# Contracting every matmul of an attention-and-expert kernel over 64 partitions, in two row tiles at once

## The chip, the cores and the metric

The kernel runs on one core of a Trainium2 chip. The metric is the device time of one execution in microseconds (us). Every time given for a kernel is the median of all its executions, slow ones included. A run called "fast" here is one within 1.5% of the fastest of the same kernel; ratios use fast runs alone.

The engines are named as the profile names them: PE is TensorE's matmuls, PEld its weight loads, ACT is ScalarE, DVE is VectorE, POOL is GpSimd, SP is the engine that issues DMA transfers. A matmul multiplies a stationary operand (loaded by a weight-load instruction; the page of the kernel after counts 9098 of each) with a moving one. Both lie across the partitions that it contracts over, 128 or 64 in these kernels, called rows below. A "64-row" matmul uses one half of them, and two of them in opposite halves run at once in these traces (they start 3 to 4 nanoseconds apart, and a pair of 512 columns takes 216, as long as one 128-row matmul): those halves are the two row tiles of the title.

## The reference

```python
# q, k, v: (batch 8, heads 8, sequence 1152, head 64), float32
q_pool = q.reshape(B, H, S // 2, 2, D).mean(axis=3)            # 576 queries per head
scores = (q_pool @ k.transpose(0, 1, 3, 2)) / np.sqrt(D)
attn   = softmax(scores)
x      = (attn @ v).transpose(0, 2, 1, 3).reshape(4608, 512)
out    = np.maximum(x @ w1, x @ w2) @ w_out                    # 512 -> 1024 -> 512
```

The kernels use max(a, b) = relu(a - b) + b: with wd = w1 - w2 and w21 = w2 @ w_out, computed once, the second part is relu(x @ wd) @ w_out + x @ w21. It is called the expert part below.

## The kernel before

The kernel records all its operations in one list, in an order chosen by a small planner at build time, and then emits each engine's share. An operation waits on semaphores for what it depends on. Two heads (a "head pair") are handled together, 32 pairs in all.

Three kinds of TensorE work matter here. The scores contract over the head's 64 elements, so they always used 64 rows: head 0 of the pair in the upper half, head 1 in the lower, side by side.

```python
sps = [psum([P, 2, 512], f"sps{g}") for g in range(3)]     # three score buffers
fb  = [psum([P, 512], f"fb{g}") for g in range(2)]         # two "lanes" for all other work

def one(e, half, t, lo, n, col):                           # scores
    h = half * 64
    return e.matmul(sps[r][:, half, col:col + n],
                    kT[ks][h:h + 64, t, :], qpT[qs][h:h + 64, lo:lo + n], start=True, stop=True)
...
# ScalarE: one exponential of 128 x 1024 per key tile (nine of them, and two rest groups)
return e.activation(eta[es][:, :, g, :], sps[r][:, :, :], EXP, scale=scale)
```

The value matmuls (attention times v, with a column of ones for the row sums, 65 columns) and the two expert layers (mostly 512 columns) contract over all 128 partitions:

```python
def chunk(half, sb):                                       # values: 9 matmuls of 65 columns
    def go(e, m):
        for t in range(NT):
            last = e.matmul(fb[m][:, sb * 66:sb * 66 + 65],
                            eta[es][:, half, t, sb * P:(sb + 1) * P], vE[vs][:, t, half, 0:65],
                            start=(t == 0), stop=(t == NT - 1))
        return last
...
last = e.matmul(fb[m][:, 0:size], wd[:, ct, ft * P:(ft + 1) * P], xT[:, ct, n0:n1],
                start=(ct == 0), stop=(ct == NC_ - 1))     # expert layer 1; layer 2 is alike
```

While attention runs, the planner puts scores first, in bursts of two or three groups, and fills the gaps with value and expert units. What of the expert part is left when the scores are done is the "tail".

The softmax here doesn't subtract the row's maximum and nothing guards it: scores larger than these inputs give would overflow.

Of the kernel before, what the change touches and what calls it, by code (L numbers as in the profile page):

```python
# [9 lines left out]
EXP = mybir.ActivationFunctionType.Exp  # L10
ALU = mybir.AluOpType


class Plan:

# [28 lines left out]
    def when(self, eng, r=(), w=(), after=()):  # L44

        t = self.free.get(eng, 0.0)
        for d in self.deps(r, w, after)[0]:
            p = self.ops[d]
            if p["eng"] != eng or p["dma"] is not None:
                t = max(t, p["seen"] + 0.05)  # L50
        return t

    def op(self, eng, fn, r=(), w=(), dma=None, cost=0.1, mode="f", after=(), solo=False):
# [7 lines left out]
        t = self.when(eng, r, w, after)  # L61
# [4 lines left out]
        else:  # L66
            if eng == "PE" and mode != self.mode:
# [5 lines left out]
                             seen=seen, end=self.free[eng], solo=solo))  # L73
# [7 lines left out]
    def solve(self):  # L81
# [3 lines left out]
        for n, o in enumerate(ops):  # L85
# [3 lines left out]
            for d in sorted(o["deps"], reverse=True):  # L89
                p = ops[d]  # L90
                if p["dma"] is None:
                    if p["eng"] == eng and (eng == "PE" or d not in o["raw"]):
                        continue
                    key = p["eng"]
                else:
                    key = ("dma", p["dma"])
                if kn.get(key, -1) >= d:
                    continue
                o["waits"].append(d)
                for k, v in p["know"].items():  # L100
                    if kn.get(k, -1) < v:
                        kn[k] = v
                kn[key] = max(kn.get(key, -1), d)
# [39 lines left out]
class Job:  # L143


    def __init__(self, kind, units, evac, done=None, nb=None):
        self.kind, self.units, self.evac, self.done = kind, units, evac, done
        self.nb = nb


def bass_funnel_attn__then__act_maxout2_kernel(
# [14 lines left out]
    QP = 64  # L166
    QU = SQ // QP
    NA = 512
    NB = SQ - NA
    NCH = NA // P  # L170
# [5 lines left out]
    NBLK = NTOK // 512  # L176
    assert D == 64 and S == NT * P and SQ == QP * QU and QU == NT and C == H * D and E == 512
    assert NB == 64 and NTOK % 512 == 0 and NT == 9
    scale = 0.5 / float(D) ** 0.5

    ctx = ExitStack()
    with ctx:
# [10 lines left out]
        qp = [sbuf([QP, QU, 2, D], BF16, f"qp{s}") for s in range(2)]  # L193
# [4 lines left out]
        eta = [sbuf([P, 2, NT, NA], BF16, f"eta{s}") for s in range(2)]  # L198
        etb = [sbuf([P, NT, 2, NB], BF16, f"etb{s}") for s in range(2)]
        rc = [sbuf([P, 6], FP32, f"rc{s}") for s in range(2)]  # L200
# [13 lines left out]
        osb = [stage[:, NC_ * F + s * E:NC_ * F + (s + 1) * E] for s in range(3)]  # L214

        sps = [psum([P, 2, 512], f"sps{g}") for g in range(3)]
        fb = [psum([P, 512], f"fb{g}") for g in range(2)]

        plan = Plan()
        op = plan.op  # L220

# [19 lines left out]
        def load_q(i):  # L241
# [3 lines left out]
                q[b, h0:h0 + 2, :, :].rearrange("h (p r) d -> (h p) (r d)", p=QP)),  # L245
# [22 lines left out]
        def cast_q(i):  # L268
            s, r = i % 2, i % 3
            for half in range(2):  # L270
                a = qraw[r][half * QP:half * QP + QP, :, :, :]
                op("POOL", lambda g, half=half, a=a: g.tensor_tensor(  # L272
                    qp[s][:, :, half, :], a[:, :, 0, :], a[:, :, 1, :], ALU.add),
                    r=[f"qraw{r}"], w=[f"qp{s}.{half}"], cost=1.4,
                    solo=half == 1)
# [7 lines left out]
        def unit(r, cost, go, mode="f"):  # L283

            def plan_it(m):
                op("PE", lambda e: go(e, m), r=r, w=[f"f{m}"], cost=cost, mode=mode)
            return r, plan_it, cost
# [4 lines left out]
        def qtrans(i):  # L292
            s = i % 2

            def go(e, m):
                mb = fb[m][:, :].bitcast(BF16)
                for u in range(QU):
                    last = e.transpose(  # L298
                        mb[:, u * QP:(u + 1) * QP],
                        qp[s][:, u, :, :].rearrange("p h d -> p (h d)"), ident[0:QP, 0:QP])  # L300
                return last

            def evac(m):
                mb = fb[m][:, :].bitcast(BF16)
                dve(lambda e: e.tensor_copy(qpT[s][:, :], mb[:, 0:SQ]),
                    [f"f{m}"], [f"qpT{s}", f"f{m}"], 0.4)
            return Job("q", [unit([f"qp{s}.0", f"qp{s}.1", "ident"], 0.3, go, "s")], evac, ("q", i))

        def ktrans_pe(i):
            s = i % 2  # L310
            v3 = i % 3
            jobs = []
            for lo, hi in ((0, 5), (5, NT)):
                def go(e, m, lo=lo, hi=hi):
                    mb = fb[m][:, :].bitcast(BF16)
                    for t in range(lo, hi):
                        last = e.transpose(
                            mb[:, (t - lo) * P:(t - lo + 1) * P],
                            kbf[s][:, t, :, :].rearrange("p h d -> p (h d)"), ident[:, :])
                    return last  # L320

                def evac(m, lo=lo, hi=hi):
                    mb = fb[m][:, :].bitcast(BF16)
                    dve(lambda e: e.tensor_copy(
                        kT[v3][:, lo:hi, :].rearrange("p t x -> p (t x)"),
                        mb[:, 0:(hi - lo) * P]),
                        [f"f{m}"], [f"kT{v3}", f"f{m}"], 0.7)
                jobs.append(Job("q", [unit([f"kbf{s}", "ident"], 0.055 * (hi - lo), go)], evac,
                                ("k", i) if lo else None))
            return jobs  # L330

        def av_jobs(i):
# [6 lines left out]
            def chunk(half, sb):  # L339
                def go(e, m):  # L340
                    for t in range(NT):
                        last = e.matmul(  # L342
                            fb[m][:, sb * 66:sb * 66 + 65],
                            eta[es][:, half, t, sb * P:(sb + 1) * P],
                            vE[vs][:, t, half, 0:65],
                            start=(t == 0), stop=(t == NT - 1))
                    return last
                return unit([f"eta{es}.{t}" for t in range(NT)] + [f"vE{vs}"], 0.275, go)

            def rest():  # L350
                def go(e, m):
                    for t in range(NT):
                        last = e.matmul(  # L353
                            fb[m][:, 4 * 66:4 * 66 + 131],
                            etb[es][:, t, :, :].rearrange("p h c -> p (h c)"),
                            vE[vs][:, t, :, :].rearrange("p h c -> p (h c)")[:, 0:131],
                            start=(t == 0), stop=(t == NT - 1))
                    return last
                return unit([f"etb{es}.{NT}", f"etb{es}.{NT + 1}", f"vE{vs}"], 0.53, go)

            def norm(half):
                def evac(m):
                    n = 6 if half == 0 else 4
                    c = c0 + half * D
                    a = fb[m]
                    dve(lambda e: e.reciprocal(  # L366
                        rc[half][:, 0:n],
                        a[:, 0:n * 66].rearrange("p (j c) -> p j c", c=66)[:, :, 64:65]),
                        [f"f{m}"], [f"rc{half}"], 0.13)
                    dve(lambda e: e.tensor_tensor(  # L370
                        xnat[xs][:, 0:NCH, c:c + D],
                        a[:, 0:NCH * 66].rearrange("p (j c) -> p j c", c=66)[:, :, 0:D],
                        rc[half][:, 0:NCH].unsqueeze(2).to_broadcast([P, NCH, D]),
                        ALU.mult),
                        [f"f{m}", f"rc{half}"],
                        [f"xn{xs}.{j}.{h0 + half}" for j in range(NCH)]
                        + ([f"f{m}"] if half else []), 0.38)
                    if half == 0:
                        dve(lambda e: e.tensor_scalar_mul(
                            xnat[xs][0:64, NCH, c:c + D], a[0:64, 264:264 + D],  # L380
                            rc[0][0:64, 4:5]), [f"f{m}", "rc0"], [f"xn{xs}.{NCH}.{h0}"], 0.2)
                        dve(lambda e: e.tensor_scalar_mul(  # L382
                            xnat[xs][0:64, NCH, c + D:c + 2 * D], a[64:P, 330:330 + D],
                            rc[0][64:P, 5:6]), [f"f{m}", "rc0"],
                            [f"xn{xs}.{NCH}.{h0 + 1}", f"f{m}"], 0.2)
                return evac

            last = ("x", b) if i % NHP == NHP - 1 else None
            return [
                Job("a", [chunk(0, sb) for sb in range(NCH)] + [rest()], norm(0)),  # L390
                Job("a", [chunk(1, sb) for sb in range(NCH)], norm(1), last)]
        gcount = [0]

        def scores(i, g):
# [3 lines left out]
            r = gcount[0] % 3  # L398
            gcount[0] += 1

            def one(e, half, t, lo, n, col):
                h = half * 64
                return e.matmul(  # L403
                    sps[r][:, half, col:col + n],
                    kT[ks][h:h + 64, t, :],
                    qpT[qs][h:h + 64, lo:lo + n],
                    start=True, stop=True)

            if g < NT:
                def pe(e):  # L410
                    one(e, 0, g, 0, NA, 0)
                    return one(e, 1, g, 0, NA, 0)

                def act(e):
# [494 lines left out]
```

## Time and profile before

The median was 418.46 us in the runs before the change (414.5 to 418.68).

| reading | value |
|---|---|
| span of the profiled execution | 415.9 us |
| PE busy | 379.6 us (91%) |
| ACT busy | 314.4 us (76%) |
| first exponential starts, last ends | 13.1 us, 341.7 us |
| tail after the last exponential | 74 us |
| steps between 64-row and 128-row matmuls, in the built order | 321 |

Three parts of the page of the kernel before: busy time of each engine with its instructions; two DMA queues (packets, MB, share of 16 engines' time); the chain of work that ended last.

```profile
PE 379.6 (91%) x4846; PEld 203.6 (49%) x4905; DVE 156.3 (38%) x355; ACT 314.4 (76%) x370; POOL 164.9 (40%) x136
...
q1 hardware_dynamic: 81552, 85.05, 74.0%
q8 instruction: 38, 0.62, 0.6%
...
PE 80%; DVE 8%; ACT 6%; issue 2%; DMA 1%; POOL 1%; another core or an unknown queue 0%
```

TensorE is the limit: it is busy 91% of the time and holds 80% of the chain. q8 is the queue whose packets the profile calls "instruction", 38 in the whole run.

The stretches view of the kernel before: window, its length, busy us (and instructions) of PE, PEld, DVE, ACT, POOL, then the granted TensorE clock, the DMA share and GB/s.

```profile
100.00:200.00 100.00, 96.86 (x1333) 50.97 (x1349) 36.51 (x90) 91.58 (x106) 48.63 (x38) 1.00 0.79 209
200.00:300.00 100.00, 96.69 (x1416) 53.18 (x1435) 38.45 (x96) 93.55 (x110) 50.66 (x40) 1.00 0.96 255
...
342.00:416.00 74.00, 67.64 (x393) 31.66 (x399) 20.46 (x36) 8.60 (x17) 0.00 (x0) 1.00 0.32 67
```

During attention both TensorE (97%) and ScalarE (92 to 94%) are near full; then TensorE works alone for 74 us.

The timeline of PE, 201 to 204 us: start, length, line and operation, number of matmuls. (L342 values, L403 scores, L581 expert layer 2.)

```profile
201.26 1.26 PE L342 MATMUL fb<-vE,eta 128*128 128x65 bf16 x36
202.46 0.82 PE L403 MATMUL sps<-qpT,kT 64*128 64x512 bf16 x6
203.44 0.38 PE L581 MATMUL fb<-w,xT 128*128 128x512 bf16 x1 [0.16 <-issue]
203.65 1.13 PE L342 MATMUL fb<-vE,eta 128*128 128x65 bf16 x32
```

This is the pattern that the change attacks: TensorE goes from 128 rows (L342) to 64 rows (L403) and back. In the records of this trace each such step costs about 94 nanoseconds (ns) more than a step without it (a value matmul is followed by a score matmul after 125 ns instead of 30). What TensorE does in these 94 ns, the trace doesn't show.

Two lines of the waits view of the kernel before: who waited for what, total us, times, longest.

```profile
ACT eta L415 <- PE sps L403: 34.3, 31, 11.1
...
PEld fb L342 <- issue: 14.4, 34, 0.8
```

ScalarE is starved for 34 us in all, 11.1 of them at the start. Idle time put down to "issue" (nothing that the profile shows was being waited for) never lasts over 0.8 us on TensorE.

### The profile page before, as it was taken

The page shows a single profiled execution, that of the slowest core. Times are in us where ns is not written, and L with a number is a line of the kernel's source. Part 1 is how long each engine was busy: PE and PEld are TensorE (multiplying, and loading weights), DVE is VectorE, ACT ScalarE, POOL GpSimd, SP SyncE. Part 2 cuts the span into 40 slices and gives each one's busy share as a digit, 9 for nine tenths or more (in the row PEclk, how much of TensorE's full clock was granted, in tenths as well). Part 3 has the DMA queues.
Part 4 walks back from the last instruction along what each step waited for, and adds up shares of the span by engine and source line. Part 5 has one row for each costly group of instructions (what it writes and reads, how often), then busy time and mean ns, then how long its engine had stood idle before and what let it go on. Part 6 is the DMA issues. An engine that isn't in the chain of part 4 may idle for free.

```text
span 415.9 us, 11123 instructions
## 1 busy us (share of the span) xinstructions
PE 379.6 (91%) x4846; PEld 203.6 (49%) x4905; DVE 156.3 (38%) x355; ACT 314.4 (76%) x370; POOL 164.9 (40%) x136
## 2 busy tenths in 40 slices
PE   0787897899999999999999999999999999999996
PEld 0355544545365536545555545555555554344442
DVE  1224738344233533244334433344333444432210
ACT  1788997899989997999799999999999980011121
POOL 5982643654346534644165536452751000000000
PEclk9988998999999999999999999999999999999999
DMA  8999997796499949974999899849964203423223
GB/s 297 403 401 391 401 283 182 155 333 159 78 344 249 277 91 315 328 225 59 303 283 240 131 307 305 267 64 325 296 138 93 46 2 65 96 50 76 64 61 66
DMA packets 81600, 85.76 MB, mean 206 GB/s; under 512 B 54416, under 2 KB 54416, under 8 KB 81552
## 3 DMA queue, kind: packets, MB, share of 16 engines
q1 hardware_dynamic: 81552, 85.05, 74.0%
q8 instruction: 38, 0.62, 0.6%
q14 instruction: 10, 0.08, 0.1%
HBM read 62.91 MB, written 9.44 MB: 174 GB/s over the span
## 4 chain that ended last, share of the span: by engine, by line
PE 80%; DVE 8%; ACT 6%; issue 2%; DMA 1%; POOL 1%; another core or an unknown queue 0%
PE fb L581 23%; PE fb L342 17%; PE sps L403 17%; PE fb L549 15%; ACT eta L415 5%; PE fb L353 4%; PE fb L298 2%; DVE wd L488 2%; PE fb L516 1%; DVE stage L598 1%; DMA qraw<-in_q_dram 1%; DVE xnat L370 1%; DVE xnat L382 1%; DVE wo L483 1%; POOL qp L272 1%
## 5 line engine op out<-in xcount | busy, mean ns | idle before, releaser
L415 ACT ACTIVATE eta<-sps 128x1024 bf16<-128x1024 f32 x288 | 269.6, 1047 | 35.0 <-PE sps L403 34.3
L272 POOL TENSOR_TENSOR qp<-qraw 64x576 bf16<-64x576 f32 x64 | 90.8, 1419 | 60.9 <-PE fb L298 54.2
L403 PE MATMUL sps<-qpT,kT 64*128 64x64 bf16 (+1 forms) x1152 | 104.6, 290 | 7.3 <-ACT eta L415 5.5
L342 PEld LDWEIGHTS fb<-vE,eta 128*128 128x128 bf16 x2304 | 79.4, 98 | 37.3 <-issue 14.4
L342 PE MATMUL fb<-vE,eta 128*128 128x65 bf16 x2304 | 88.7, 194 | 6.1 <-DVE xnat L382 3.1
L549 PE MATMUL fb<-xT,wd 128*128 128x512 bf16 (+2 forms) x304 | 76.3, 358 | 3.1 <-issue 1.3
L581 PE MATMUL fb<-wo,stage 128*128 128x512 bf16 (+1 forms) x275 | 76.5, 380 | 1.7 <-issue 1.0
L564 DVE TENSOR_SCALAR stage<-fb 128x512 bf16<-128x512 f32 (+2 forms) x68 | 44.4, 656 | 69.4 <-PE fb L549 69.0
L403 PEld LDWEIGHTS sps<-qpT,kT 64*128 64x128 bf16 x1152 | 31.2, 94 | 54.2 <-ACT eta L415 27.6
L279 POOL TENSOR_SCALAR vE<-vraw 128x1152 bf16<-128x1152 f32 x32 | 37.3, 1165 | 47.7 <-issue 35.0
L257 POOL TENSOR_SCALAR kbf<-kraw 128x1152 bf16<-128x1152 f32 x31 | 36.7, 1184 | 48.0 <-DMA kT<-kbf 47.3
L366 DVE RECIPROCAL rc<-fb 128x6 f32<-128x6 f32 x64 | 12.1, 189 | 114.0 <-PE fb L353 71.7
L549 PEld LDWEIGHTS fb<-xT,wd 128*128 128x128 bf16 x320 | 25.3, 97 | 37.2 <-DVE stage L564 6.0
L558 ACT ACTIVATE stage<-fb 128x288 bf16<-128x288 f32 (+1 forms) x12 | 5.7, 473 | 50.0 <-PE fb L549 50.0
L581 PEld LDWEIGHTS fb<-wo,stage 128*128 128x128 bf16 (+1 forms) x296 | 26.0, 98 | 30.3 <-issue 7.4
L581 PE MATMUL fb<-w,xT 128*128 128x512 bf16 (+1 forms) x130 | 37.3, 381 | 3.3 <-DVE stage L598 1.4
L427 ACT ACTIVATE etb<-sps 128x1024 bf16<-128x1024 f32 x64 | 38.8, 673 | 0.2
L598 DVE COPY stage<-fb 128x512 f32<-128x512 f32 (+1 forms) x32 | 22.1, 690 | 31.4 <-PE fb L581 31.1
L370 DVE TENSOR_TENSOR xnat<-fb,rc 128x256 bf16<-128x256 f32 x64 | 27.2, 424 | 2.2
L353 PE MATMUL fb<-vE,etb 128*128 128x131 bf16 x288 | 23.1, 226 | 0.0
L298 PE MATMUL fb<-ident,qp 64*128 64x64 bf16 x288 | 14.0, 192 | 9.8 <-POOL qp L272 8.8
L298 PEld LDWEIGHTS fb<-ident,qp 64*128 64x128 bf16 x288 | 10.7, 96 | 19.6 <-POOL qp L272 8.8
(27 smaller groups left out, 113.7 us busy)
## 6 DMA issues: line engine op xcount, KB each, us to landing
qraw<-in_q_dram SPq DMA_DIRECT2D x32, 576.0 KB, 7.0
kraw<-in_k_dram SPq DMA_DIRECT2D x32, 576.0 KB, 5.9
vraw<-in_v_dram SPq DMA_DIRECT2D x32, 576.0 KB, 8.1
out_dram<-stage SPq DMA_DIRECT2D x72, 128.0 KB, 2.5
xT<-in_moe_w_dram SPq DMA_DIRECT2D x1, 2048.0 KB, 15.6
stage<-in_moe_w_out_dram SPq DMA_DIRECT2D x1, 2048.0 KB, 19.3
stage<-in_moe_w_dram SPq DMA_DIRECT2D x1, 2048.0 KB, 17.4
xT<-xnat SPq DMA_TRANSPOSE x40, 2.5
```

The source lines that it names most:

```text
L257: op("DVE" if i == 0 else "POOL", lambda g: g.tensor_scalar(kbf[s][:, :, :, :].rearrange("p t h d -> p h t d"), kraw[r][:, :, :, :], 1.0, ...
L272: op("POOL", lambda g, half=half, a=a: g.tensor_tensor(qp[s][:, :, half, :], a[:, :, 0, :], a[:, :, 1, :], ALU.add), r=[f"qraw{r}"], w=[f" ...
L279: op("POOL", lambda g: g.tensor_scalar(vE[r][:, :, :, 0:D].rearrange("p t h d -> p h t d"), vraw[r][:, :, :, :], 1.0, 1.0, ALU.mult, ALU.m ...
L298: last = e.transpose(mb[:, u * QP:(u + 1) * QP], qp[s][:, u, :, :].rearrange("p h d -> p (h d)"), ident[0:QP, 0:QP])
L342: last = e.matmul(fb[m][:, sb * 66:sb * 66 + 65], eta[es][:, half, t, sb * P:(sb + 1) * P], vE[vs][:, t, half, 0:65], start=(t == 0), stop ...
L353: last = e.matmul(fb[m][:, 4 * 66:4 * 66 + 131], etb[es][:, t, :, :].rearrange("p h c -> p (h c)"), vE[vs][:, t, :, :].rearrange("p h c -> ...
L403: return e.matmul(sps[r][:, half, col:col + n], kT[ks][h:h + 64, t, :], qpT[qs][h:h + 64, lo:lo + n], start=True, stop=True)
L415: return e.activation(eta[es][:, :, g, :], sps[r][:, :, :], EXP, scale=scale)
L427: return e.activation(etb[es][:, t0:t0 + n, :, :].rearrange("p t h c -> p h t c"), sps[r][:, :, 0:n * NB].rearrange("p h (t c) -> p h t c" ...
L549: last = e.matmul(fb[m][:, 0:size], wd[:, ct, ft * P:(ft + 1) * P], xT[:, ct, n0:n1], start=(ct == 0), stop=(ct == NC_ - 1))
L564: dve(lambda e: e.tensor_scalar_max(gT[:, ft, g0:g0 + size], fb[m][:, 0:size], 0.0), [f"f{m}"], [f"gT.{g0 // 64}.{ft}", f"f{m}"], 0.1 + si ...
L581: last = e.matmul(fb[m][0:hi - lo, :], lhs, rhs, start=(j == 0), stop=(j == NC_ + NF - 1))
```

## The change

The intent: if every matmul uses 64 rows, TensorE never changes its mode (none of the 94 ns steps), and two halves at once do the work of one 128-row matmul (216 ns at 512 columns, for a pair as for one). Each unit is split into pairs: lane m has two banks, bank x takes half x in the first phase and the other half in the second, where the first phase's sum is added to. The kernel lets the second phase wait until the first has written (`own`, a wait of TensorE on itself).

```diff
-    def op(self, eng, fn, r=(), w=(), dma=None, cost=0.1, mode="f", after=(), solo=False):
+    def op(self, eng, fn, r=(), w=(), dma=None, cost=0.1, mode="f", after=(), solo=False,
+           own=None):
...
+        if own is not None:
+            deps.add(own)
...
-        sps = [psum([P, 2, 512], f"sps{g}") for g in range(3)]
-        fb = [psum([P, 512], f"fb{g}") for g in range(2)]
+        sps = [psum([P, 2, 512], f"sps{g}") for g in range(2)]
+        fb = [psum([P, 2, 512], f"fb{g}") for g in range(2)]
...
-            def chunk(half, sb):
+            def chunk(sb, ph, first):
+                n = P if sb < NCH else NB
+
                 def go(e, m):
                     for t in range(NT):
-                        last = e.matmul(
-                            fb[m][:, sb * 66:sb * 66 + 65],
-                            eta[es][:, half, t, sb * P:(sb + 1) * P],
-                            vE[vs][:, t, half, 0:65],
-                            start=(t == 0), stop=(t == NT - 1))
+                        for x in range(2):
+                            half = rows(x ^ ph)
+                            a = t * SQ + sb * P
+                            last = e.matmul(
+                                fb[m][0:n, x, sb * 66:sb * 66 + 65],
+                                et[es][half, x, a:a + n], vE[vs][half, t, x, 0:65],
+                                start=(first and t == 0), stop=(not first and t == NT - 1))
                     return last
...
+        def two(r, cost, go):                  # the expert layers: the same two phases
+
+            def phase(ph):
+                def run(e, m):
+                    for x in range(2):
+                        last = go(e, fb[m][:, x, :], x, x ^ ph, ph)
+                    return last
+                return unit(r, cost, run)
+            return phase
...
-                            last = e.matmul(
-                                fb[m][:, 0:size], wd[:, ct, ft * P:(ft + 1) * P],
-                                xT[:, ct, n0:n1],
-                                start=(ct == 0), stop=(ct == NC_ - 1))
+                        return e.matmul(a[:, 0:size], wd[rows(half), ct, f:f + P],
+                                        xT[rows(half), ct, n0:n1],
+                                        start=(ph == 0 and ct == 0), stop=(ph == 1 and ct == NC_ - 1))
```

The scores are cut into eleven groups of about 942 elements per partition instead of nine of 1024 with two rests. There are two score buffers instead of three, and the lanes hold four banks instead of two. The planner issues one group at a time instead of bursts. The diff's remainder (transposes in halves, another order of tokens, queues of the planner) isn't needed below.

In the built order TensorE's matmuls go from 4905 to 9098, its row-mode steps from 321 to 0.

## The prediction

> **What bounds it now.** The chain of waits puts 80% of the span on TensorE, which is 91% busy. The stretches view shows two regimes: to 342 us attention runs with ScalarE near full (91.6 of 100 us between 100 and 200) while TensorE fills in expert work; the last 74 us are TensorE's alone. Both limits are close: exponentials of 128x1024 start every 0.91 us (records), so all 352 need about 296 us after the first at 13.1 us; the last ends at 341.7, 32 us above that floor.
>
> **TensorE's account, from start-to-start times in the records.** 512-column matmuls follow each other in 216 ns, 65-column value matmuls in 29 to 31 ns; two score matmuls in opposite row halves start 3 ns apart, and such a pair takes 216 ns at 512 columns, 29 ns at 64. Each step between a 64-row and a 128-row matmul costs more: L342 to L403 takes 125 ns instead of 30, L581 to L403 311 instead of 216. That is about 94 ns per switch. [...]
>
> **What the change does.**
> - Removes: in the built order TensorE switches row mode 321 times before, 0 after: 321 x 0.094 = 30 us.
> - Doubles matmuls (4905 to 9098), but in concurrent pairs. Values: 90 pairs x 29.3 ns = 2.64 us per head pair against 2.78 now (72 x 31 + 9 x 61 ns). Experts: a 512-column pair takes what a 128-row matmul took. Estimated sum of pure TensorE work: 328 us against 337. [...]
> - Equal groups: same elements (942 per row, estimated 0.84 us each from the slope between the 1024 and 128 forms), same count of 352; ScalarE's floor stays near 296 us.
> - Adds: a wait of each job's second phase on its own first (about 0.23 us from a matmul's start to what it releases), hidden only if the other lane has work; two score buffers instead of three; two-bank evacuations (about 1.2 us instead of 0.69); 0.5 us more at the very end.
>
> **On the critical path.** Work behind the last scores in the order falls from about 67.6 to 48.3 us, if the attention stage doesn't stretch. That stage holds 280 us of TensorE work instead of 270 + 28 of switches, so it gains 10 to 18 us, until ScalarE (13 + 296 + early gaps of 15 to 20 = 325 to 330 us) limits. I expect the last exponential near 328 us, then 48 us of work, 6 us of bubbles, 3.5 us of ending: about 385 us.
>
> **Predicted: 384 us, 8 in 10 between 370 and 402. Faster by over 2%: 0.93; within 2%: 0.05; slower: 0.02.**
>
> **What would show it.** Value pairs at 29 to 31 ns; no 94 ns steps; 52 to 60 us after the last exponential instead of 74; last exponential at 320 to 335 us; ScalarE busy 88 to 93% until then; TensorE waiting on itself under 10 us in total.
>
> **What would make it wrong.** Sustained value pairs slower than 29 ns because four instructions per 29 ns can't be issued for long [...]; self-waits left uncovered; expert lanes blocked by two-bank evacuations; ScalarE starved by two score buffers in early head pairs.

Three passages that no trace of this case shows are cut from the text above. 328 us to the last exponential, 48 of work, 6 of bubbles and 3.5 of ending come to 385.5 us ("about 385"). That value pairs keep 29.3 ns was the estimate from 64-column pairs in the trace of before, seen only in runs of eight or nine pairs. The 0.84 us for an exponential were one too, from start-to-start times of 904 ns at 1024 elements and about 158 at 128, and so were the 1.2 us for a two-bank evacuation (one of 1024 elements, L619, took 1.19 us in the kernel after). That four instructions per 29 ns can't be issued for long was named as a risk; no trace had shown it.

## The result, and the profile after

The kernel after took **457.89 us** in the median (four runs, 457.6 to 458.58), the kernel before 417.91 us in the same rounds. The ratio is 1.098 (95% interval 1.091 to 1.104): almost 10% slower, where 8% faster was predicted. (A ratio here is the mean time of one kernel's fast runs over that of the other's of the same rounds, so it isn't quite the ratio of the medians quoted.)

The same parts of the page, for the kernel after:

```profile
PE 392.2 (86%) x9098; PEld 249.3 (55%) x9098; DVE 134.2 (29%) x278; ACT 325.1 (71%) x363; POOL 163.1 (36%) x136
...
q1 hardware_dynamic: 81552, 85.05, 66.3%
q8 instruction: 71, 1.16, 1.1%
...
PE 83%; issue 8%; ACT 5%; DVE 1%; DMA 1%; POOL 1%
```

TensorE is less busy, and "issue" now holds 8% of the chain, some 37 us of 457. The instruction queue moved 71 packets instead of 38.

The stretches view of the kernel after, columns as above:

```profile
100.00:200.00 100.00, 89.71 (x2170) 56.92 (x2168) 29.34 (x62) 82.57 (x92) 40.58 (x32) 0.96 0.73 197
200.00:300.00 100.00, 89.00 (x2142) 58.13 (x2138) 27.93 (x61) 79.45 (x89) 39.33 (x32) 0.93 0.73 203
...
398.00:457.00 59.00, 51.51 (x770) 28.67 (x766) 12.74 (x19) 6.92 (x11) 0.00 (x0) 0.99 0.31 65
```

The tail is what was predicted, 59 us instead of 74. The loss is all in attention: the last exponential ends at 398 us instead of 342. Both engines that should be near full there have idle time, TensorE 10 to 11% and ScalarE 17 to 21%, and the granted clock is below 1.

The waits view of the kernel after shows the idle time of ScalarE, then of PE and of PEld:

```profile
ACT et L437 <- PE sps L428: 74.8, 81, 10.1
...
PE fb L377 <- issue: 28.8, 19, 3.3
...
PEld fb L377 <- issue: 37.4, 47, 3.4
...
PEld fb L567 <- PE fb L567: 14.3, 39, 0.6
PEld fb L377 <- PE fb L377: 10.9, 54, 0.4
```

ScalarE's starvation doubles from 34 to 75 us. The last two lines are TensorE's waits on itself, 25 us here (27 us with a third group at L600; an account of the records gave 26), each short. The two above them are something else: 19 times ahead of a value matmul and 47 times ahead of a value weight load (the same stops, and shorter ones) TensorE stood still, up to 3.4 us, with nothing to wait for.

One of these stops, in the timeline of PE of the kernel after:

```profile
285.81 0.70 PE L377 MATMUL fb<-vE,et 64*128 64x65 bf16 x36
286.35 0.36 PE L428 MATMUL sps<-qpT,kT 64*128 64x472 bf16 x2
286.58 0.23 PE L377 MATMUL fb<-vE,et 64*128 64x65 bf16 x4
289.53 1.20 PE L377 MATMUL fb<-vE,et 64*128 64x65 bf16 x32 [2.71 <-issue]
```

A value unit (18 matmuls; two units are 36) breaks off after its fourth matmul, in the middle of a straight run of instructions of which only the first can have a wait. It goes on 2.7 us later. ScalarE pays for it in its own timeline:

```profile
282.30 5.53 ACT L437 ACTIVATE et<-sps 128x944 bf16<-128x944 f32 x6
291.71 0.95 ACT L437 ACTIVATE et<-sps 128x940 bf16<-128x940 f32 x1 [3.89 <-PE sps L428]
```

The 3.89 us of idle time are put down to the scores, but the scores were late because TensorE stood still.

Where do these stops lie? TensorE's instructions have records (weight loads, matmuls and some semaphore instructions, in program order; 59 matmul records are missing in the kernel before, none in the kernel after), so they can be counted. A stop is counted where two records start over 0.3 us apart and the second has no wait; its length is that distance. This is worked out from the records, not a view of the profile:

```
                                                  before      after
TensorE records                                     9846      18288
instruction packets (16,384 bytes each)               38         71
stops that end 1.15-1.75 us after such a packet:
  count, sum                                   2, 0.6 us  27, 39.3 us
positions of the 27 in the program            24 of them at record 193 modulo 256
one packet takes (median)                                  1.0 us
resume after the end of a packet (median)                  1.43 us
```

18288 records over 71 packets are 258 for each packet. One packet for every 256 instructions fits that, and the stops repeat with exactly that period. (Why the remainder is 193 isn't shown.) That the stops end just after a packet isn't an effect of the window chosen: of all 22 such distances over 0.45 us in the kernel after, not one lies outside it. For the stop shown: TensorE passed the preceding border at 283.65 us; the packet that ended the stop moved from 286.98 to 287.95; the last instruction before the border at 286.62; it resumed at 289.53. So that packet's transfer started 3.3 us after the preceding border was passed, and 0.36 us after TensorE had already reached the next one.

What the DMA engines did in that stretch, 283 to 292 us, in the DMA view (packets, MB, the sum of the packets' times as a share of 16 engines' time):

```profile
q1 hardware_dynamic: 2913, 2.88, 109.3%
q8 instruction: 1, 0.02, 0.7%
```

They were full with the loads of q, k and v of later head pairs.

### The profile page after: what moved, and what is told of

It reads as the page before. It is cut to its first block, busy times and chain, and to the rows that moved or that the text cites. A ratio compares the mean times of both kernels' runs of the same rounds, so it can differ in the third digit from the quotient of the medians.

```text
span 456.9 us, 19468 instructions
## 1 busy us (share of the span) xinstructions
PE 392.2 (86%) x9098; PEld 249.3 (55%) x9098; DVE 134.2 (29%) x278; ACT 325.1 (71%) x363; POOL 163.1 (36%) x136
## 4 chain that ended last, share of the span: by engine, by line
PE 83%; issue 8%; ACT 5%; DVE 1%; DMA 1%; POOL 1%
PE fb L377 25%; PE fb L600 23%; PE sps L428 16%; PE fb L567 15%; ACT et L437 5%; PE fb L531 2%; PE fb L329 2%; DMA qraw<-in_q_dram 1%; POOL qp L299 1%; PE fb L347 0%; DVE stage L619 0%; DVE w L536 0%; ACT stage L616 0%; DVE stage L579 0%; DVE kT L355 0%
## 5 line engine op out<-in xcount | busy, mean ns | idle before, releaser
L437 ACT ACTIVATE et<-sps 128x944 bf16<-128x944 f32 (+1 forms) x352 | 317.0, 957 | 79.1 <-PE sps L428 74.8
L377 PE MATMUL fb<-vE,et 64*128 64x65 bf16 (+1 forms) x5760 | 140.1, 194 | 31.8 <-issue 28.8
L428 PE MATMUL sps<-qpT,kT 64*128 64x472 bf16 (+8 forms) x1216 | 142.0, 294 | 14.1 <-ACT et L437 8.6
L377 PEld LDWEIGHTS fb<-vE,et 64*128 64x128 bf16 (+1 forms) x5760 | 116.5, 99 | 65.0 <-issue 37.4
L567 PE MATMUL fb<-xT,wd 64*128 64x512 bf16 (+3 forms) x704 | 92.2, 351 | 2.6 <-issue 1.3
L600 PE MATMUL fb<-wo,stage 64*128 64x512 bf16 (+1 forms) x608 | 88.2, 377 | 0.0
L579 DVE TENSOR_SCALAR stage<-fb 128x1024 bf16<-128x1024 f32 (+3 forms) x38 | 41.7, 1098 | 60.7 <-PE fb L567 60.7
L567 PEld LDWEIGHTS fb<-xT,wd 64*128 64x128 bf16 x704 | 33.6, 96 | 32.4 <-PE fb L567 14.3
L600 PE MATMUL fb<-w,xT 64*128 64x512 bf16 (+1 forms) x304 | 46.0, 372 | 0.8 <-DVE stage L579 0.4
L600 PEld LDWEIGHTS fb<-wo,stage 64*128 64x128 bf16 x608 | 32.2, 96 | 19.8 <-issue 0.8
L619 DVE COPY stage<-fb 128x1024 f32<-128x1024 f32 (+1 forms) x15 | 17.8, 1189 | 44.9 <-PE fb L600 44.9
L329 PEld LDWEIGHTS fb<-ident,qp 64*128 64x128 bf16 x288 | 12.8, 99 | 12.0 <-POOL qp L299 8.6
L600 PEld LDWEIGHTS fb<-w,xT 64*128 64x128 bf16 x304 | 12.9, 94 | 10.1 <-PE fb L600 1.8
```

The lines of the kernel that those rows point to most:

```text
L329: last = e.transpose(mb[:, u * HP:(u + 1) * HP], qp[s][:, u, :, :].rearrange("p h d -> p (h d)"), ident[0:HP, 0:HP])
L377: last = e.matmul(fb[m][0:n, x, sb * 66:sb * 66 + 65], et[es][half, x, a:a + n], vE[vs][half, t, x, 0:65], start=(first and t == 0), stop= ...
L428: last = e.matmul(sps[r][:, h, n0 - a:n1 - a], kT[ks][rows(h), t, :], qpT[qs][rows(h), n0 - t * SQ:n1 - t * SQ], start=True, stop=True)
L437: op("ACT", lambda e: e.activation(et[es][:, :, a:z], sps[r][:, :, 0:z - a], EXP, scale=scale), r=[f"s{r}"], w=[f"et{es}.{g}", f"s{r}"], c ...
L567: return e.matmul(a[:, 0:size], wd[rows(half), ct, f:f + P], xT[rows(half), ct, n0:n1], start=(ph == 0 and ct == 0), stop=(ph == 1 and ct ...
L579: dve(lambda e: e.tensor_scalar_max(gT[:, f0:f0 + 2, g0:g0 + size], fb[m][:, :, 0:size], 0.0), [f"f{m}"], w + [f"f{m}"], 0.1 + size / 480.0)
```

## Theories

**Theory A, instruction supply.** TensorE's instructions come in blocks of 256, one for each packet on the instruction queue, and where a block comes too late TensorE stands at its border. The records of the kernel after show the order: all 71 packets start between 1.0 us before and 5.4 us after the border of the same number (records 193, 449 and so on) was passed, and 24 of the 27 stops lie at the border after that one. A pair of value matmuls with its two weight loads is four instructions in 30 ns, so 256 of them are used up in 1.9 us at that pace (an estimate), and the densest blocks in the records, with score and expert work in between, took 2.5 to 3.0 us. From passing a border to going on after the next one it takes the start delay, about 1.0 us for the packet and 1.4 us until TensorE resumes. At the stop shown, with the DMA engines full, the start delay was 3.3 us, and the sum 5.9 us. Over the whole run the stops come to 39 us.

**The rivals.** The added waits of TensorE on itself (some 26 us); the two-bank lanes; value pairs that run slower when sustained; the coarser order: one group at a time with two score buffers, value units bunched at the start of a head pair; TensorE's clock, which its records show at half for about 47 us instead of 13. Each expectation below says which it sets against A; the letters other than A there stand for these rivals.

## The experiments

"Stops" below means the sum of stops that end 1.15 to 1.75 us after an instruction packet, as counted above (39.3 us in the kernel after). Each group was run on one chip with its own runs of the kernel before: medians 418.11, 417.26 and 417.15 us.

### Fewer loads: the kernel after, and the kernel before

From the fourth head pair on only 8 of 128 partitions of q, k and v are loaded. The result is wrong on purpose; engines do the same work.

```diff
-                kraw[s][:, :, :, :].rearrange("p h t d -> p h (t d)"),
-                k[b, h0:h0 + 2, :, :].rearrange("h (p t) d -> p h (t d)", t=NT)),
+                kraw[s][0:(P if i < 3 else 8), :, :, :].rearrange("p h t d -> p h (t d)"),
+                k[b, h0:h0 + 2, :, :].rearrange("h (p t) d -> p h (t d)", t=NT)[0:(P if i < 3 else 8), :, :]),
     # q and v alike; the same edit in the kernel before is the control
```

> The changed kernel, same instructions in the same order, but from the fourth head pair on each load of q, k and v brings only 8 of 128 partitions (the result is wrong on purpose), so the DMA engines are nearly idle after 40 us. Theory A (TensorE waits for its own instructions, fetched in blocks of 256 by DMA, 27 stalls and 39 us in the changed kernel[...]): the waits without a semaphore at block borders fall from 39 us to under 12 us, the clock returns to about 0.98, and the time falls to 400 to 425 us. Theory B (lanes, self-waits, two score buffers, or value pairs that run slower when sustained): these are untouched, time stays 448 to 460 us.

> Control: the same cut of the loads in the kernel before (wrong result on purpose). Theory A: the kernel before has no stalls at block borders, so it gains nothing, 410 to 420 us. If the loads slow something other than the fetch (casts, SBUF access), this kernel gains as much as the changed one, and theory A is not supported by the first run.

Measured: the kernel after falls to 423.60 us (ratio to before 1.016, interval 1.012 to 1.019), 34 us less. The control stays at 416.65 us (0.998, 0.994 to 1.002). The data queue and the stops of the kernel after without its loads:

```profile
q1 hardware_dynamic: 63456, 36.94, 40.0%
...
PE fb L377 <- issue: 10.5, 12, 3.2
```

The stops fall from 39.3 to 12.8 us, half-clock time from 47 to 22 us. That is within the range of A for the time, and just above the 12 us expected of the stops. Nothing that TensorE computes or waits for was changed; only what the DMA engines carry. The records show the step between: in the kernel after a packet starts 1.7 us after its border in the median and 4.1 us at the 90th percentile, with few loads 0.9 and 1.7 us. That supports A, and the control shows that the loads themselves don't hold up the kernel before. 12 stops remain, so fewer loads are not enough by themselves (the DMA engines were still 41% busy between 100 and 300 us, not nearly idle as expected).

### Values alone back on 128 partitions

Half as many value instructions; scores and experts stay in row tiles, so the mode steps return. The result is correct.

```diff
-            def chunk(sb, ph, first):
+            def chunk(sb, x):
...
-                        for x in range(2):
-                            half = rows(x ^ ph)
-                            a = t * SQ + sb * P
-                            last = e.matmul(... et[es][half, x, a:a + n], vE[vs][half, t, x, 0:65], ...)
+                        a = t * SQ + sb * P
+                        last = e.matmul(... et[es][:, x, a:a + n], vE[vs][:, t, x, 0:65], ...)
...
+            phases = [[chunk(sb, x) for sb in range(NCH + 1) for x in range(2)]]
```

> The changed kernel with its value matmuls back on 128 partitions (no phases, no self-wait in them): 6218 matmuls instead of 9098, 346 row-mode switches instead of 0. Theory A: stalls at block borders under 6 us; switches cost about 346 x 94 ns = 33 us again; time 405 to 425 us, near the kernel before, in spite of two score buffers and two-bank lanes. Theory B: the lanes and buffers stay as they are and the switches come on top, 450 to 490 us.

Measured: 422.94 us (1.013, 1.007 to 1.020). From its page and its waits view:

```profile
PE 390.3 (92%) x6218; PEld 240.2 (56%) x6218; DVE 135.0 (32%) x273; ACT 325.7 (77%) x368; POOL 167.3 (39%) x136
...
q8 instruction: 49, 0.80, 0.9%
...
PEld fb L375 <- issue: 31.1, 154, 0.4
...
ACT et L431 <- PE sps L422: 22.0, 18, 9.7
```

35 us less than the kernel after, although 346 mode steps are back (some 33 us at 94 ns each, an estimate). There isn't one stop at a border left: idle time without a cause is in pieces of at most 0.4 us ahead of the value weight loads. (The one longer piece, 2.2 us ahead of an expert weight load, stands behind a semaphore wait for a DMA.) ScalarE's starvation goes from 75 to 22 us and the last exponential ends at 340 us. Two score buffers, equal groups, two-bank lanes and expert self-waits are all still there, so they don't explain the starvation. (The value self-waits went with the phases; the run without self-waits, below, deals with those.)

### Experts alone back on 128 partitions

The mirror image: values stay in tiles.

```diff
-                    for x in range(2):
-                        last = go(e, fb[m][:, x, :], x, x ^ ph, ph)
-                    return last
-                return unit(r, cost, run)
+                    return go(e, fb[m][:, x, :], x, slice(0, P), 0)
+                return unit(r, cost, run, "f")
```

> The changed kernel with only its expert matmuls back on 128 partitions (value matmuls still in row tiles): 8258 matmuls, 463 switches. Theory A: the value matmuls are the dense part, so stalls at block borders stay, 25 to 45 us, and 43 us of switches come on top, self-waits of the expert jobs (about 11 us) go: 470 to 505 us. If the doubling of the expert matmuls made the stalls: 440 us or less.

Measured: 488.80 us (1.171, 1.167 to 1.174), correct, and as expected. It has 463 mode steps in the built order and still 33.8 us of stops. (82 matmul records are missing from this trace, so the positions can't be counted; the stops are told by the packets.) Together with the last experiment: the narrow value matmuls in tiles bring the stops, the wide expert matmuls in tiles alone don't.

### Value units spread out

At most one value unit per score group, so that they aren't bunched. Correct.

```diff
+                    if job.kind == "a" and nxt < min(job.at + NG, len(groups)) and 10 - job.left() > nxt - job.at:
+                        continue
```

> The changed kernel, same instructions, but a head pair's ten value units are spread one per score group instead of packed into the first groups. Theory A: blocks of 256 instructions last longer where they were shortest, so the stalls fall from 39 us to 15 to 30 us and the time to 430 to 450 us; not to zero, as the average is still about 5 us per block. Theory B (self-waits, lane blocking): spreading keeps one lane occupied all the time, so time stays or rises, 455 to 480 us.

Measured: 461.96 us (1.102, 1.095 to 1.110). This is a miss for A as it was put: the time lies in the range given to B, not in A's 430 to 450 us. The bunching as a cause falls: spread out, the kernel is no faster. That the stops would shrink fell too. They were 41.5 us, in a profile of a slow run, so only roughly comparable. So this run doesn't tell A from B by the time; the stops, still there, and the runs below do. A likely reason, not tested: under load TensorE can go on after the next border 4.1 us after it passed the one before, in the median, and 6.5 us with the 90th percentile of the start delay (sums of the parts above), and a block lasts about 5 us on average during attention (an estimate from the records, stops not counted), wherever in the head pair the value units stand.

### No waits of TensorE on itself

The halves aren't swapped between the phases, so the second phase needs no wait. Wrong on purpose (each sum covers one half twice).

```diff
-                            half = rows(x ^ ph)
+                            half = rows(x)
...
-                        last = go(e, fb[m][:, x, :], x, x ^ ph, ph)
+                        last = go(e, fb[m][:, x, :], x, x, ph)
...
-            self.own = self.last
+            self.own = None
```

> The changed kernel without the swap of row halves between the two phases of a job (each row tile keeps its own bank, so no phase waits for the one before; the sums are incomplete, the result wrong on purpose), loads as they were. In the account of the changed kernel's records the self-waits cost 26 us. Theory A plus self-waits: those go to under 2 us, but the instructions are used up faster, so the stalls at block borders grow from 39 us to 42 to 55 us and part of the gain is given back: 436 to 452 us. If the fetch did not bind: the whole 26 us, about 430 us or less. If self-waits were covered anyway: 455 to 460 us.

> The same without the phase swap, and with the loads cut to 8 partitions from the fourth head pair on (wrong on purpose). Against the 423.6 us of the run with cut loads alone: self-waits to zero, stalls 12 to 25 us, 402 to 412 us. This would leave about 20 us above the predicted 384, in remaining stalls and the half clock.

Measured: without self-waits 463.20 us (1.110, 1.103 to 1.116), and the expected gain is a miss. In the waits view, where the kernel after had 28.8 us:

```profile
PE fb L377 <- issue: 35.0, 23, 3.7
```

The stops rise from 39.3 to about 54 us. This fits A, by which the next block is on its way while TensorE waits on itself, so that without the wait TensorE arrives at the border earlier and stands there (a reading of the totals; it was not followed packet by packet). But the account doesn't close: 26 us of self-waits went, some 15 us of stops came, and the time still rose by 5 us. So self-waits cost nothing that could be measured as long as the stops are there; where the rest went stays open.

Without self-waits and with few loads: 416.83 us (0.998, 0.992 to 1.003). Here the self-waits were worth 7 us (423.60 to 416.83, across two chips). This too was expected lower, 402 to 412 us. 25.9 us of stops remain, just above the expected range, and the prediction's 384 us plus 26 us of stops plus some 9 us of value pairs slower than assumed (32.5 ns on average in this run instead of 29.3) would be 419; that sum was made after the run and isn't a test.

### The kernel before with a longer instruction stream

If A holds, the kernel before must slow down when nothing but its number of instructions grows. Each 512-column expert matmul is cut into matmuls of 64 columns: the same rows, columns, loads, buffers and order. Wrong on purpose (the sums of a bank are restarted).

```diff
-                        for j in (2 * kk, 2 * kk + 1):
+                        for c, j in [(c, 2 * kk + d) for c in range(8) for d in range(2)]:
+                            w = slice(c * 64, c * 64 + 64)
...
-                            last = e.matmul(fb[m][0:hi - lo, :], lhs, rhs,
-                                            start=(j == 0), stop=(j == NC_ + NF - 1))
+                            last = e.matmul(fb[m][0:hi - lo, w], lhs, rhs[:, w],
+                                            start=(j == 2 * kk), stop=(j == 2 * kk + 1))
     # expert layer 1 alike
```

> The kernel before, with every 512-column expert matmul cut into eight of 64 columns (same data, same waits, same schedule; wrong result on purpose as the sums are restarted): 10029 matmuls instead of 4905, as many as in the changed kernel, but with no row tiles, lanes, buffers or phases of the change. At 29.3 ns per 64 columns against 216 per 512 the slower pace alone costs about 12 us: 430 us if the instruction supply is no limit. Theory A: 256 instructions are now used up in 3.7 to 5 us at many borders, so stalls without a semaphore appear at block borders, 20 to 70 us in sum, and the time is 450 to 495 us.

Measured: 457.59 us (1.097, 1.094 to 1.099). From its page and its waits view:

```profile
PE 402.2 (88%) x10025; PEld 319.4 (70%) x10029; DVE 160.3 (35%) x355; ACT 317.6 (70%) x370; POOL 165.2 (36%) x136
...
q8 instruction: 78, 1.28, 1.2%
...
PE fb L342 <- issue: 8.4, 8, 1.9
...
PEld fb L342 <- issue: 23.2, 42, 2.0
```

The same kernel as before, with 10,029 matmuls instead of 4905, has stops of 26.7 us with the period of 256 (0.6 us in the kernel before), and they hit its value matmuls (L342), which were not touched, as well as the cut ones. The time is within the range of A. About 12 us of the rest are the slower pace of eight narrow matmuls against one wide (an estimate from start-to-start times). So stops come without row tiles, self-waits, two-buffer scores or the new order. That the total equals that of the kernel after is chance. It was half-clocked for only 12.4 us, as long as the kernel before (12.8), so the slow clock isn't needed for the stops either.

### Loads in smaller parts

Each load of 576 KB is split in four, given out over the score groups, to leave the instruction queue gaps. Correct.

```diff
+            for a, z in parts if part is None else [parts[part]]:
+                op("SP", lambda e, a=a, z=z: e.dma_start(
+                    kraw[s][a:z, ...], k[b, h0:h0 + 2, ...][a:z, ...]), w=[f"kraw{s}.{a}"], ...)
...
+            for _ in range(2 if len(slow_load) > 10 else 1):     # after each score group
+                if slow_load:
+                    fn, i, part = slow_load.pop(0)
+                    fn(i, part)
```

> The changed kernel (right result) with each 576 KB load of q, k and v issued as four of 144 KB, one or two per score group instead of all at the start of a head pair; same bytes. Theory A[...]: the packet of a fetch starts sooner after its border (90th percentile 2 to 3 us instead of 4.1), stalls fall from 39 to 20 to 32 us, time 435 to 452 us. If only the amount of traffic counts, not its bursts: 455 to 460 us.

Measured: 481.96 us (479.80 in the three fast ones of five runs; 1.146, 1.142 to 1.151), clearly slower and a miss. The data queue:

```profile
q1 hardware_dynamic: 86160, 85.07, 85.3%
```

It took 85% of the engines' time instead of 66% for the same bytes, fetches started 5.0 us (90th percentile) after a border instead of 4.1 us, and the stops rose to 55.9 us, where 20 to 32 us were expected (this profile fell in a slow run). So the parts are dearer to move, and the DMA engines are busy for 70% or more of each of the first 32 of the 40 slices of the page (in the kernel after some of these fall to 20%). It agrees with A, but shows nothing about bursts, since it raised the load itself; that a fetch stands behind bursts was a supposition. Why four parts take longer than one wasn't tested.

### Towards a better version

The lesson so far: narrow matmuls on 128 partitions, wide ones in tiles. Three kernels, all correct, build on "values on 128 partitions". The first lets value units run on in bursts, for fewer mode steps (190 instead of 346). The second also does the expert work of the tail on 128 partitions without phases. The third has shorter bursts and tells the planner that an exponential takes 0.86 us instead of 0.9.

```diff
+            go_on = [kk for kk in (0, 1) if plan.mode == "f" and lane[kk] is not None
+                     and lane[kk].kind == "a" and now() + 0.4 <= t_buf + SLACK]
+            if go_on:                                # SLACK 0.9; third kernel 0.8
+                emit_unit(go_on[0])
...
+        def phases_of(steps, full):                  # second and third kernel: full in the tail
+            if full:
+                return [[s(x) for s in steps for x in range(2)]]
+            return [[s(ph) for s in steps] for ph in range(2)]
```

> The version with value matmuls on 128 partitions (422.9 us, 346 switches) with the value units of a head pair run in longer bursts: the next scores may come up to 0.9 us after their buffer is free. 190 switches instead of 346, so 15 us less of switching; ScalarE starves a little more in each burst. Expected 405 to 420 us, no stalls at block borders. If switches were not what that version pays, 420 to 430 us.

> The version before this, and the expert jobs built after the last scores run on 128 partitions without phases, so without self-waits (6 us in the records of that stage) and with half the instructions. Expected 3 to 8 us less than the run before: 400 to 415 us, below the kernel before (418).

> Variant of the version at 413 us: value units on 128 partitions in bursts, scores allowed to be 0.8 us late instead of 0.9, the planner's exponential set to 0.86 us (measured spacing 0.84), last expert jobs on 128 partitions: 251 switches instead of 191 (5.6 us more), less starving of ScalarE (waits for it fall from 27 to about 20 us). Expected 408 to 417 us, no stalls at block borders.

Measured: 416.42 us (0.997, 0.992 to 1.003) for the first; one of its four runs took 754.63 us, was the profiled one, and stays unexplained, so its profile isn't used. The second took **413.16 us** (0.991, 0.985 to 0.996), the third 413.47 us (0.990, 0.987 to 0.993), all in their expected ranges. Both are about 1% faster than the kernel before. The second has no stops at all, the third 0.6 us. What is left of the change's gain is small. That the mode steps were only made fewer may be why, but it isn't shown: 156 steps less, estimated at 15 us, brought 6.5 us in the first kernel (across two chips), and ScalarE's starvation was 44 us in the second and 29 us in the third, at the same time.

## Why the prediction was wrong, point by point

**Right.**
- No mode steps: 0 of 321 left, and no 94 ns steps in the records.
- The tail: 59 us after the last exponential, predicted 52 to 60.
- The exponentials: about 0.84 us from start to start when fed, as estimated. (But ScalarE was fed only 80% of the time until the last one; 88 to 93% was predicted.)
- The pace of value pairs: 30 ns in the median, predicted 29 to 31.

**Wrong: the sum of the attention stage.** The prediction put "pure TensorE work: 328 us", "That stage holds 280 us of TensorE work instead of 270 + 28 of switches, so it gains 10 to 18 us", and the last exponential "near 328 us" (320 to 335). It ended at 398 us. The step that failed is taking the time of TensorE's work for the time of the stage. Here the two parted where instructions came later than TensorE could use them. That term was missing from the sum, and the experiments show it: 39 us of stops at block borders, which vanish with half the value instructions, shrink with a quiet DMA, and appear in the kernel before when its stream is lengthened. They are the largest part of the 70 us by which the last exponential came late, not all of it (see the account below).

**Wrong: the self-waits.** "TensorE waiting on itself under 10 us in total" was 26 us. Removing it gained nothing with all loads (463.20 us), but 7 us when loads were few.

**The risk named, but not in the right place.** "Four instructions per 29 ns can't be issued for long", a supposition, pointed at the instruction stream. But the pace held (30 ns a pair in the median); the supply broke off, at 24 of the 71 block borders, for up to 3.45 us. And a 2% chance for slower was far too little for a change that almost doubles instructions (9846 to 18288 records) on an engine busy 91% of the time. The trace of before held what was needed: a packet of 256 instructions takes about 1 us and starts some 1.8 us (median) to 3.5 us (90th percentile) after a border (with the places of the missing records filled in), and pairs at 29 ns, four instructions each, use up 256 instructions in about 2 us by estimate, with the score and expert work between them in 2 to 3 us.

A rough account of 458 against 384 us, worked out from the records of the kernel after; the parts overlap and were not measured one by one:

```
stops at block borders                                              39 us
self-waits (overlap with the stops; removing them gained 0 or 7 us)  up to 26 us
value pairs: mean 33 ns instead of 29.3, 2880 pairs                 about 10 us
half-clock time (about 47 us instead of 13), estimated loss         about  6 us
```

The last two overlap as well: in half-clock time a value pair takes 55 ns in the median instead of 30, and those pairs are part of the mean of 33 ns.

In the clock records of this trace the half-clock stretches are 3.4 or 6.8 us long (the last, at the end of the run, 2.8 us). 9 of the 12 begin within 2 us of the end of a stop of 2.2 to 3.45 us, or during it (one of these stops, of 2.2 us, ended at an instruction with a wait). So most of the slow clock comes with or after the stops; what brings it on wasn't tested. It is a small part: the lengthened kernel before has 26.7 us of stops with no more of it (12.4 us against 12.8).

**Open.** How many blocks are fetched ahead and by which rule (that the packet which ends a stop starts only after the preceding border was passed is all that was seen). Why value pairs average over 32 ns with a median of 30 even outside half-clock time. Where the rest went in the run without self-waits. Why the split loads kept the DMA engines busier. The one run of 754 us.

## What to carry to other kernels

Count instructions like any other resource: splitting a matmul into two concurrent row tiles cost no array time here (a pair of 512 columns took 216 ns, as one did before) but twice the instructions, so before splitting, compare the time in which 256 instructions of the densest stretch are used up (here 2.5 to 3 us) with the time that a block needs to arrive after the border before it (sums of the parts above: about 3.3 us with few loads, 4.1 us in the median and 6.5 us at the 90th percentile with all loads). Keep narrow matmuls on all 128 partitions (here 422.94 us, against 457.89 with the value matmuls in tiles). Tiles for the wide ones brought no stops here, but little gain either, 1% at best. Long idle pieces that a profile puts down to "issue" on a straight run of instructions are a sign of it: look whether they repeat with a fixed period and end a fixed time after an instruction packet.
